# Where the low parts of one weight chunk wait, and split products for six down chunks of the last token block

## The chip, the core and the metric

The kernel runs on one core of a Trainium2 chip. The metric is the device time of one execution in microseconds (us). A core has five engines that run their own instruction queues in order and meet at semaphores: PE (TensorE, the matrix unit), DVE (VectorE), ACT (ScalarE), POOL (GpSimd) and SP (SyncE, which issues DMAs here). PEld is the row of the profile for PE's weight loads.

## The reference

Two stages, one after the other:

```python
def phi(x):                                   # x: (4, 4, 1088, 32), S1, S2: (8, 32)
    a = einsum('rd,bhsd->bhsr', S1, x); b = einsum('rd,bhsd->bhsr', S2, x)
    return einsum('bhsi,bhsj->bhsij', a, b)   # 64 features
q_p, k_p = phi(q), phi(k)
num = q_p @ (k_p^T v);  den = q_p @ sum(k_p) + 1e-6
x = (num / den), heads side by side           # (4352 tokens, 128)
g = x @ w_gate;  val = x @ w_val              # 128 -> 1536
out = (g * sigmoid(g) * val) @ w_out          # 1536 -> 128
```

The feed-forward part is what this text is about: for every block of tokens, 1536 hidden columns in 12 chunks of 128, each made by a gate and a value product, and then a down product of each chunk with `w_out`, summed over the 12 chunks.

## The kernel before, in words

Tokens are cut into blocks: three of batch 0 (numbers 0, 1, 2, of 384, 320 and 384 tokens), then `line`, six blocks of 480 and a last one, `LAST`, of 384. A unit (i, j) is chunk j of block i: gate and value product, silu on ACT, and on DVE the product of both into a slot of `hbuf` (or `late`). A down (i, j) multiplies that slot by chunk j of `w_out` into a PSUM bank that gathers the block's 12 chunks. `todo` holds the units whose down is still to come.

Blocks 0 and 1 use plain float32 products (line 1016). From block 2 on the gate and value products are split: an operand is cut into parts that fit float32r, one matmul instruction each, and a product is the sum of three. The weights' parts are made by `cut_weights` (line 839), a generator that does one step each time it is advanced: `w1` on ACT (line 843); the low part `low = w - w1` into room lent to it, on POOL or DVE (line 846); `wb`, the scaled low part, on ACT (line 848); `wd`, their difference, on POOL or DVE (lines 851, 855). Four chunks of three (0 to 3) of `wg` and `wv` are cut, under the names g0 to g3 and v0 to v3; g0 and v0 use POOL. `steps_at` tables (lines 1307, 1328, 1343, 1355) say by hand after which unit or down each step is issued. A unit of a split block is `start_unit` (line 974: two matmuls with `wd`, then ACT rescales both banks in place, line 983) and `finish_unit` (line 985: four matmuls, lines 992 and 993, silu at line 995, DVE's product at line 1000). Three PSUM pairs serve these units; `let_go` frees one after line 1000.

Around the first edit: in lines 1333 to 1340 thirteen downs are issued (`ND`), with cuts between them; lines 1347 to 1353 run units (2, 6) to (2, 11), one unit ahead on PE, with one down after each and one step of batch 1's attention (`parts_of`, lines 377, 741 to 758). That attention ends in `phT`, which PE needs at line 776 before the next blocks' tokens exist. v0's low part goes to `room[:, 6]` and g0's to `room[:, 8]`, which are free long before; ACT instructions and POOL instructions are queued in the order in which the program issues them.

Around the second edit: `DOWN` (lines 888, 889) lists the downs that are split as well: six of `line[2]` and eight each of `line[3:6]`. For such a unit `cut_hidden` (line 942) makes three parts of the hidden chunk: h1 one step later (ACT, line 959, or DVE, line 957), h0 two steps later on POOL (line 960), hd three steps later on DVE (line 963). `before` and `behind` are lists by step y that `finish_unit` runs at its begin and at its end. `down` (line 1045) then issues three float32r matmuls (lines 1060, 1062, 1063) in place of one plain float32 product, which is two instructions (line 1068). The sum of the `wd` products and the plain chunks lies in one bank; the other two parts lie in a second bank `p`, which ACT copies to SBUF (`copy_out`, line 1081) and DVE joins with the first (`put_together`, line 1088, line 1092). In a block with split downs the plain chunks use `scaled`, a copy of `-w_out` (line 930) that holds the seven chunks in `PLAIN`. `LAST` has none of this: its downs cover 256 tokens (`SPLIT`), all plain, and are stored by a DVE transpose (line 1113) and four DMAs on two queues; the other 128 tokens are done by `straight` (line 1097), the operands exchanged, at the very end, and leave through `o_last`.

The loop over `line` (lines 1381 to 1399) issues at step y the start of unit y+1, the finish of unit y and up to two downs:

```python
        for _ in range(2):
            if len(todo) > min(5 + (todo[0] == (line[1], 0)), END - y + 1):
                down(y)
```

Of the kernel before, what the change touches and what calls it, by code (L numbers as in the profile page):

```python
# [12 lines left out]
AF = mybir.ActivationFunctionType  # L13
# [6 lines left out]
def kernel(  # L20
# [818 lines left out]
    def cut_weights(w, c, low, engine):  # L839

        w1, wb, wd = w_parts[id(w), c] = home(w, c)
        src = w[:, 3 * c : 3 * c + 3, :]
        nc.scalar.activation(out=w1, in_=src, func=AF.Copy, scale=CUT)
        yield
        low = low[0]
        engine.tensor_tensor(out=low, in0=src, in1=whole(w1), op=ALU.subtract)
        yield
        nc.scalar.activation(out=wb, in_=low, func=AF.Copy, scale=BETA)
        yield
        if engine is nc.vector:  # L850
            nc.vector.scalar_tensor_tensor(
                out=wd, in0=low, scalar=-BETA, in1=whole(w1), op0=ALU.mult, op1=ALU.add
            )
        else:
            engine.tensor_tensor(out=wd, in0=whole(w1), in1=whole(wb), op=ALU.subtract)

    def cut_tokens(i, engine=nc.gpsimd, soon=False):

        t0, n = blocks[i]
        x = xT[:, t0 : t0 + n]  # L860
        x1, x0, xd = x_parts[i] = [
            apool.tile([P, WB], F32R, tag=tag, name=name, bufs=2)
            for tag, name in (("qb", "x1"), ("dT", "x0"), ("rd", "xd"))
        ]
        nc.scalar.activation(x1[:, 0:n], x, AF.Copy, scale=CUT)  # L865

        def low():
            engine.tensor_tensor(  # L868
                out=x0[:, 0:n], in0=x, in1=whole(x1[:, 0:n]), op=ALU.subtract
            )  # L870

        def difference():
            nc.vector.scalar_tensor_tensor(
                out=xd[:, 0:n], in0=whole(x1[:, 0:n]), scalar=WHOLE, in1=x,
                op0=ALU.mult, op1=ALU.subtract,
            )


        first, second = (difference, low) if soon else (low, difference)
        first()  # L880
        yield
        second()
# [1 line left out]


    line = list(range(HEAD, len(blocks)))
    FINE, PLAIN = range(1, NCH - 1), (0, 1, 3, 5, 7, 6, NCH - 1)
    DOWN = [(line[2], j) for j in (2, 4, 6, 8, 9, 10)]
    DOWN += [(i, j) for i in line[3:6] for j in (1, 2, 4, 5, 7, 8, 9, 10)]
    down_parts = {}  # L890
    h_parts = {}
    h_sets = []
# [2 lines left out]
    def add_to(where, y, f):  # L895
        where.setdefault(y, []).append(f)
# [5 lines left out]
    def cut_down():  # L902

        n = len(FINE)
        parts = const.tile([P, 3, n, D], F32R, tag="room", name="dparts", bufs=1)
        w1, wb, wd = (parts[:, k] for k in range(3))
        scaled = apool.tile([P, len(PLAIN), D], FP32, tag="zs", name="scaled")
        low = const.tile([P, n, D], FP32, tag="late", name="dlow", bufs=1)
        down_parts.update(w1=w1, wb=wb, wd=wd, scaled=scaled)
        rest = [(0, slice(0, 1)), (1, slice(1, 8, 2)), (5, slice(6, 7)), (6, slice(NCH - 1, NCH))]  # L910

        def high(c):
            nc.scalar.activation(w1[:, c], wo[:, FINE[0] :][:, c], AF.Copy, scale=CUT)

        def left(c):
            nc.gpsimd.tensor_tensor(
                out=low[:, c], in0=wo[:, FINE[0] :][:, c], in1=whole(w1[:, c]), op=ALU.subtract
            )

        def scale(c):  # L920
            nc.scalar.activation(wb[:, c], low[:, c], AF.Copy, scale=BETA)

        def differ(c):
            nc.gpsimd.tensor_tensor(
                out=wd[:, c], in0=whole(w1[:, c]), in1=whole(wb[:, c]), op=ALU.subtract
            )

        def other(k, c):
            m = len(range(NCH)[c])
            nc.scalar.activation(scaled[:, k : k + m, :], wo[:, c, :], AF.Copy, scale=-1.0)  # L930

        a, b, c = slice(0, 3), slice(3, 6), slice(6, n)
        for step in (
            [(high, a)], [(left, a), (high, b)], [(left, b), (scale, a)], [(differ, a), (high, c)],
            [(left, c), (scale, b)], [(differ, b), (scale, c)], [(differ, c), (other, *rest[0])],
            [(other, *rest[1])], [(other, *rest[2]), (other, *rest[3])],
        ):
            for f, *args in step:
                f(*args)
            yield  # L940

    def cut_hidden(y, i, j):

        if not h_sets:
            x = []
            for tag in ("kld", "qld", "vld", "kT", "qT"):
                t = const.tile([P, 2, WB], F32R, tag=tag, name="h" + tag, bufs=1)
                x += [t[:, k, :] for k in range(2)]
            t = const.tile([P, 8, WB], F32R, tag="late", name="hlate", bufs=1)
            x += [t[:, k, :] for k in range(8)]  # L950
            h_sets.extend(x[k : k + 3] for k in range(0, 18, 3))
        n = blocks[i][1]
        h_sets.append(h_sets.pop(0))
        h1, h0, hd = h_parts[i, j] = [x[:, 0:n] for x in h_sets[-1]]
        h = hidden[i, j][:, 0:n]
        if j in (2, 5, 8, 10) and i != line[2]:
            add_to(before, y + 1, lambda: nc.vector.tensor_scalar(h1, h, CUT, None, op0=ALU.mult))
        else:
            add_to(behind, y + 1, lambda: nc.scalar.activation(h1, h, AF.Copy, scale=CUT))
        add_to(before, y + 2, lambda: nc.gpsimd.tensor_tensor(  # L960
            out=h0, in0=h, in1=whole(h1), op=ALU.subtract
        ))
        add_to(before, y + 3, lambda: nc.vector.scalar_tensor_tensor(
            out=hd, in0=whole(h1), scalar=WHOLE, in1=h, op0=ALU.mult, op1=ALU.subtract
        ))
# [115 lines left out]
    def copy_out(y, i, n):  # L1081

        x = fpool.tile([P, WB], FP32, tag="sg", name="sum2", bufs=5)[:, 0:n]
        p = acc[i, "p"][:, 0:n]
        acc[i, "p"] = x
        add_to(behind, y + 1, lambda: nc.scalar.activation(x, p, AF.Copy, scale=WHOLE))

    def put_together(y, i, n):

        d, x = acc.pop(i)[:, 0:n], acc.pop((i, "p"))  # L1090
        acc[i] = x
        add_to(before, y + 1, lambda: nc.vector.scalar_tensor_tensor(
            out=x, in0=d, scalar=-1.0, in1=x, op0=ALU.mult, op1=ALU.add
        ))
        add_to(before, y + 2, lambda: store(i, n))

    def straight(ps, j):

# [10 lines left out]
    def store(i, n):  # L1109
        t0 = blocks[i][0]  # L1110

        o = fpool.tile([P, WB // 32, 32], FP32, tag="o", name="o", bufs=2)
        nc.vector.transpose(
            out=o[:, 0 : n // 32, :], in_=acc.pop(i)[:, 0:n].rearrange("p (x t) -> p x t", t=32)
        )
        t1 = t0 + n
        while t0 < t1:
            b, x0 = divmod(t0 // 32, NX)
            m = min(t1 - t0, S * (b + 1) - t0) // 32
            k = (t0 - blocks[i][0]) // 32  # L1120
            for a in range(4):
                queue = nc.scalar if i == LAST and a % 2 else nc.sync
                queue.dma_start(
                    out=rows[b, a, :, x0 : x0 + m, :],
                    in_=o[32 * a : 32 * a + 32, k : k + m, :],
                )
            t0 += 32 * m
# [106 lines left out]
    def parts_of(n):  # L1234

        for _ in range(n):
            if ahead[0] not in ("pe", "end"):
                ahead[0] = next(att, "end")
# [37 lines left out]
    def free(c):  # L1276
        return [room[:, c, :].rearrange("p (c f) -> p c f", f=P)]
# [11 lines left out]

    cuts = {"x": cut_tokens(2, nc.vector, soon=True)}
    for c in (2, 3, 0, 1):
        cuts["g%d" % c] = cut_weights(wg, c, free(8 + c % 2), nc.vector if c else nc.gpsimd)
        cuts["v%d" % c] = cut_weights(wv, c, free(6 + c % 2), nc.vector if c == 1 else nc.gpsimd)

    def at(*names):
        for name in names:
# [9 lines left out]
    for z, (i, j) in enumerate(seq):  # L1308
# [18 lines left out]

    steps_at = {
        0: ("g2", "v2", "v3"), 1: ("g2",), 2: ("g2", "g3"), 3: ("g3", "v2"), 4: ("g3", "v3"), 5: ("g2",),
        7: ("x",), 8: ("x", "g3", "v0"), 9: ("g0",), 10: ("v0",), 11: ("g0",),  # L1330
    }
    ND = 13
    for n in range(ND):
# [7 lines left out]


    steps_at = {
        9: ("v0",), 10: ("g0", "v0"), 11: ("g0", "v1", "g1", "v1", "g1"),
    }
    todo.sort(key=lambda x: (order + [x]).index(x))
    for j in range(6, NCH):
        if j + 1 < NCH:
            start_unit(2, j + 1)
        finish_unit(2, j)  # L1350
        next_down()
        parts_of(1)
        at(*steps_at.get(j, ()))
    x_steps = iter(())
    steps_at = {9: ("v1", "g1"), 8: ("v1", "g1")}
# [87 lines left out]
```

## Time and profile before

| | us |
|---|---|
| median of 3 runs (277.64 to 278.03) | 277.65 |
| the profiled execution's own time | 278.16 |
| its span, first to last instruction | 276.5 |
| PE busy in the span | 269.2 |
| DVE busy | 208.4 |
| ACT busy | 189.9 |
| POOL busy | 97.1 |

All is one execution's profile. The span lies inside the measured time: 278.16 - 276.5 = 1.66 us lie around it. A line of the timeline gives start, duration, engine, source line and operation, output and inputs with shape, and in brackets how long the engine stood idle before it and which instruction ended that. A line of the chain gives start, length and what the chain passed through, followed back from the last instruction. Two numbered records make one plain float32 matmul; in a timeline, a matmul's record begins when PE takes it, so that neighbours overlap, and the chain shows the steps without overlap.

### The profile page before, as it was taken

What the parts mean: (1) busy time and instruction counts of PE and PEld (TensorE: products, weight loads), DVE (VectorE), ACT (ScalarE), POOL (GpSimd) and SP (SyncE); (2) the same over time, 40 slices, a digit from 0 to 9 for tenths busy, and PEclk for the clock granted to TensorE, in tenths of its full rate; (3) what the DMA queues carried; (4) which work ended last, traced back from release to release, by engine and by line L of the source; (5) the groups of instructions that cost most, each with busy time, mean ns of one, the idle gap of its engine ahead of it and who ended that gap; (6) DMA issues with size and microseconds to landing.
All of it is one profiled execution on the core that took longest, in us unless ns stands there. A gap on an engine that the chain in (4) does not pass through costs nothing.

```text
span 276.5 us, 5719 instructions
## 1 busy us (share of the span) xinstructions
PE 269.2 (97%) x2181; PEld 199.9 (72%) x2181; DVE 208.4 (75%) x360; ACT 189.9 (69%) x337; POOL 97.1 (35%) x107
## 2 busy tenths in 40 slices
PE   6989999999999999999999999999999999999995
PEld 6645566667785786777577777867887888788994
DVE  2997988989998773887545666967978995987431
ACT  2468666462685686677479898768879878886860
POOL 3323422149611540260043353435425553542000
PEclk9999999999999999999999999999999999999999
DMA  6573196222231043000200020000100200010011
GB/s 190 171 206 93 53 271 195 63 100 63 58 92 20 4 115 94 2 0 0 38 13 4 1 38 0 0 2 13 24 2 0 36 1 0 17 21 0 11 29 29
DMA packets 26139, 14.30 MB, mean 52 GB/s; under 512 B 19840, under 2 KB 24192, under 8 KB 26112
## 3 DMA queue, kind: packets, MB, share of 16 engines
q1 hardware_dynamic: 25456, 13.84, 19.7%
q8 instruction: 17, 0.28, 0.4%
q10 hardware_dynamic: 656, 0.10, 0.2%
q14 instruction: 10, 0.08, 0.1%
HBM read 11.41 MB, written 2.23 MB: 49 GB/s over the span
## 4 chain that ended last, share of the span: by engine, by line
PE 91%; DVE 4%; DMA 2%; issue 1%; ACT 1%; SPq 0%
PE PS L1068 21%; PE PS L980 14%; PE PS L992 14%; PE PS L993 13%; PE PS L1016 12%; PE PS L1063 2%; PE PS L1060 2%; PE PS L1062 2%; PE PS L354 2%; PE PS L776 2%; PE PS L342 2%; DMA kld<-in_k_dram 2%; PE PS L388 2%; PE PS L1099 1%; PE PS L497 1%
## 5 line engine op out<-in xcount | busy, mean ns | idle before, releaser
L983 ACT ACTIVATE PS<-PS 128x960 f32<-128x960 f32 (+1 forms) x90 | 83.3, 925 | 33.7 <-PE PS L980 32.8
L1000 DVE SCALAR_TENSOR_TENSOR hbuf<-PS,sg 128x480 f32<-128x480 f32 (+1 forms) x87 | 55.3, 635 | 43.9 <-ACT sg L995 41.1
L995 ACT ACTIVATE sg<-PS 128x480 f32<-128x480 f32 (+1 forms) x90 | 49.6, 551 | 2.1 <-PE PS L993 1.2
L1068 PE MATMUL PS<-hbuf,wo 128*128 128x480 f32 (+3 forms) x118 | 45.8, 488 | 0.0
L980 PE MATMUL PS<-xd,graw 128*128 128x480 f32 (+1 forms) x69 | 38.2, 554 | 0.0
L993 PE MATMUL PS<-x,wb 128*128 128x480 f32 (+1 forms) x90 | 33.5, 372 | 0.0
L980 PE MATMUL PS<-xd,wd 128*128 128x480 f32 (+1 forms) x90 | 33.5, 372 | 0.0
L992 PE MATMUL PS<-x,w 128*128 128x480 f32 (+1 forms) x90 | 33.4, 371 | 0.0
L1068 PEld LDWEIGHTS PS<-hbuf,wo 128*128 128x128 f32 x118 | 22.0, 189 | 5.6 <-issue 0.4
L993 PE MATMUL PS<-x,graw 128*128 128x480 f32 (+1 forms) x69 | 25.5, 370 | 0.0
L980 PEld LDWEIGHTS PS<-xd,wd 128*128 128x128 f32 x90 | 17.0, 189 | 10.5 <-issue 6.0
L1016 PE MATMUL PS<-xT,wg 128*128 128x384 f32 (+1 forms) x60 | 23.5, 473 | 0.1
L1016 PE MATMUL PS<-xT,wv 128*128 128x384 f32 (+1 forms) x60 | 23.2, 468 | 0.3 <-DVE wv L286 0.3
L868 POOL TENSOR_TENSOR x<-xT,x 128x480 fp32r<-128x480 f32 (+1 forms) x6 | 7.2, 1193 | 38.1 <-ACT x L865 38.1
L1020 ACT ACTIVATE sg<-PS 128x384 f32<-128x384 f32 (+1 forms) x24 | 11.2, 468 | 13.2 <-PE PS L1016 12.4
L980 PEld LDWEIGHTS PS<-xd,graw 128*128 128x128 f32 x69 | 13.0, 188 | 7.7 <-ACT PS L983 4.1
L992 PEld LDWEIGHTS PS<-x,w 128*128 128x128 f32 x90 | 16.9, 187 | 2.2
L993 PEld LDWEIGHTS PS<-x,wb 128*128 128x128 f32 x90 | 16.9, 188 | 2.1
L992 PE MATMUL PS<-x,graw 128*128 128x480 f32 (+1 forms) x48 | 18.4, 384 | 0.0
L1068 PE MATMUL PS<-hbuf,scaled 128*128 128x480 f32 x36 | 17.4, 564 | 0.0
L1016 PEld LDWEIGHTS PS<-xT,wv 128*128 128x128 f32 x60 | 11.2, 190 | 7.3 <-DVE hbuf L1031 0.8
L1016 PEld LDWEIGHTS PS<-xT,wg 128*128 128x128 f32 x60 | 10.9, 190 | 7.7 <-issue 1.1
(200 smaller groups left out, 539.2 us busy)
## 6 DMA issues: line engine op xcount, KB each, us to landing
kld<-in_k_dram SPq DMA_DIRECT2D x4, 544.0 KB, 4.7
vld<-in_v_dram SPq DMA_DIRECT2D x12, 144.0 KB, 4.3
qld<-in_q_dram SPq DMA_DIRECT2D x3, 544.0 KB, 3.6
raw<-in_moe_w_out_dram SPq DMA_DIRECT2D x4, 384.0 KB, 3.9
raw<-in_moe_w_gate_dram SPq DMA_DIRECT2D x3, 384.0 KB, 3.7
raw<-in_moe_w_val_dram SPq DMA_DIRECT2D x3, 384.0 KB, 3.5
out_dram<-o SPq DMA_DIRECT2D x16, 60.0 KB, 1.9
vld<-in_v_dram SPq DMA_DIRECT2D x4, 112.0 KB, 4.0
```

The costliest lines, as they stand in the source:

```text
L342: nc.tensor.matmul(ps[32 * a : 32 * a + 32, 96 * (c - c0) : 96 * (c - c0) + 96], qT[:, 4 * c + a, :], s123[:, a : a + H, :, :].rearrange(" ...
L354: nc.tensor.matmul(ps[32 * a : 32 * a + 64, 64 * (c - c0) : 64 * (c - c0) + 64], kT[:, c, a : a + 2, :].rearrange("p a t -> p (a t)"), s12 ...
L868: engine.tensor_tensor(out=x0[:, 0:n], in0=x, in1=whole(x1[:, 0:n]), op=ALU.subtract)
L980: nc.tensor.matmul(ps[:, k], w_parts[id(w), j // 3][2][:, j % 3, :], xd, start=True, stop=True)
L983: nc.scalar.activation(ps, ps, AF.Copy, scale=-1.0 / WHOLE)
L992: nc.tensor.matmul(ps[:, k], w1, x1, start=False, stop=False, skip_group_check=True)
L993: nc.tensor.matmul(ps[:, k], wb, x0, start=False, stop=True, skip_group_check=True)
L995: nc.scalar.activation(sg, ps[:, 0], AF.Silu, scale=WHOLE)
L1000: nc.vector.scalar_tensor_tensor(out=hj[:, 0:n], in0=ps[:, 1], scalar=WHOLE, in1=sg, op0=ALU.mult, op1=ALU.mult)
L1016: nc.tensor.matmul(o[:, 0:n], w[:, j, :], xT[:, t0 : t0 + n], start=True, stop=True)
L1020: nc.scalar.activation(sg[:, 0:n], g[:, 0:n], AF.Silu)
L1068: nc.tensor.matmul(acc[i][:, 0:n], w, hidden[i, j][:, 0:n], **sides)
```

## The change

Chunk 0 of the weights: v0's low part is no longer put into `room[:, 6]`, but into the slot of `hbuf` that the down of step j = 7 has just freed. Both lows of chunk 0, which were issued at downs 10 and 11 of the thirteen, are issued at that step; both `wb` at step 9 (g0's was at 10), both `wd` at step 10 (g0's was at 11). On POOL the order of the instructions is the same as before; v0's low part now has a wait on PE. On ACT `wb` of g0 stands one unit earlier, ahead of a rescale (line 983) and a silu (line 995).

Last block: the downs of `LAST` for chunks 1, 2, 4, 5, 6 and 7 become split ones, with h parts of 256 tokens; its plain chunks (0, 3, 8, 9, 10, 11) use `scaled`, for which chunks 8, 9 and 10 take the places of 1, 5 and 7 at step 68, by three ACT instructions. The copy of `p`, the join and the store of `LAST` are issued at once rather than one or two steps later.

```diff
-    FINE, PLAIN = range(1, NCH - 1), (0, 1, 3, 5, 7, 6, NCH - 1)
+    FINE, PLAIN = range(1, NCH - 1), [0, 1, 3, 5, 7, 6, NCH - 1]
...
+    DOWN += [(LAST, j) for j in (1, 2, 4, 5, 6, 7)]
...
+        def exchange():
+            for k, c in zip((1, 3, 4), (8, 9, 10)):
+                PLAIN[k] = c
+                nc.scalar.activation(scaled[:, k, :], wo[:, c, :], AF.Copy, scale=-1.0)
+
+        add_to(behind, NCH * 5 + 8, exchange)
...
-        n = blocks[i][1]
+        n = SPLIT if i == LAST else blocks[i][1]
         h_sets.append(h_sets.pop(0))
...
-        add_to(behind, y + 1, lambda: nc.scalar.activation(x, p, AF.Copy, scale=WHOLE))
+        copy = lambda: nc.scalar.activation(x, p, AF.Copy, scale=WHOLE)
+        if i == LAST:
+            copy()
+        else:
+            add_to(behind, y + 1, copy)
...
-        add_to(before, y + 1, lambda: nc.vector.scalar_tensor_tensor(
+        join = lambda: nc.vector.scalar_tensor_tensor(
             out=x, in0=d, scalar=-1.0, in1=x, op0=ALU.mult, op1=ALU.add
-        ))
-        add_to(before, y + 2, lambda: store(i, n))
+        )
+        if i == LAST:
+            join()
+            store(i, n)
+        else:
+            add_to(before, y + 1, join)
+            add_to(before, y + 2, lambda: store(i, n))
...
+    lows = {}
...
-        cuts["v%d" % c] = cut_weights(wv, c, free(6 + c % 2), nc.vector if c == 1 else nc.gpsimd)
+        lows["v%d" % c] = free(6 + c % 2)
+        cuts["v%d" % c] = cut_weights(wv, c, lows["v%d" % c], nc.vector if c == 1 else nc.gpsimd)
...
-        7: ("x",), 8: ("x", "g3", "v0"), 9: ("g0",), 10: ("v0",), 11: ("g0",),
+        7: ("x",), 8: ("x", "g3", "v0"), 9: ("g0",),
...
-        9: ("v0",), 10: ("g0", "v0"), 11: ("g0", "v1", "g1", "v1", "g1"),
+        7: ("v0", "g0"), 9: ("v0", "g0"), 10: ("v0", "g0"), 11: ("v1", "g1", "v1", "g1"),
...
+        if j == 7:
+            lows["v0"][:] = [slots.pop().rearrange("p (c f) -> p c f", f=P)]
         at(*steps_at.get(j, ()))
```

## The prediction

> **What bounds the kernel now.** I read the page first: PE is busy 97% of the span and the chain of work that ended last lies 91% on PE.
>
> ```profile
> PE 269.2 (97%) x2181; PEld 199.9 (72%) x2181; DVE 208.4 (75%) x360; ACT 189.9 (69%) x337; POOL 97.1 (35%) x107
> ...
> PE 91%; DVE 4%; DMA 2%; issue 1%; ACT 1%; SPq 0%
> ```
>
> So an edit pays only where it shortens PE's own work or closes a hole in it. Then I read the chain in the two stretches that the edits touch. First, units (2, 6) to (2, 11), 72 to 98 us:
>
> ```profile
> 80.32 0.55 PE PS L1068 x2
> 80.87 0.01 issue
> 80.88 0.56 DVE late L1000
> ...
> 83.16 0.14 DVE phq L377
> 83.30 1.35 issue
> 84.66 0.54 DVE late L1000
> 85.20 0.90 DVE phT L758
> 86.10 0.04 issue
> 86.14 1.55 PE PS L776 x38
> ```
>
> Up to 80.87 the chain is PE's, 1.58 a unit; from there to 86.14 it is DVE's, through the attention features (line 377) and their transpose (line 758), and PE's line 776 waits for that. PE's timeline tells what the hole costs: its last four downs end at 83.08 + 2.74 = 85.82, line 776 starts at 86.14, idle 0.32. That is the most the first edit can give. Why DVE is late is in its timeline and POOL's:
>
> ```profile
> 72.80 1.29 DVE L1040 TENSOR_TENSOR hbuf<-hbuf,room 128x320 f32<-128x320 f32 x1
> ...
> 79.78 0.95 DVE L377 TENSOR_TENSOR phq<-qab 128x768 f32<-128x768 f32 x1
> ...
> 83.09 1.65 DVE L377 TENSOR_TENSOR phq<-qab 128x768 f32<-128x768 f32 x1
> ```
>
> ```profile
> 71.14 1.32 POOL L846 TENSOR_TENSOR room<-wv,w 128x384 f32<-128x384 f32 x1
> 72.43 1.31 POOL L846 TENSOR_TENSOR room<-wg,gphq 128x384 f32<-128x384 f32 x1
> 81.34 1.01 POOL L855 TENSOR_TENSOR wd<-w,wb 128x384 fp32r<-128x384 f32 x1 [7.59 <-ACT wb L848]
> 82.92 1.00 POOL L855 TENSOR_TENSOR gphq<-gphq 128x384 fp32r<-128x384 f32 x1 [0.57 <-ACT gphq L848]
> ```
>
> The same instruction of line 377 takes 0.95 alone and 1.65 beside g0's `wd` (82.92 to 83.92). It ends at 84.74 and all behind it is 0.70 late. Second, the last block, in the chain from 254 us on:
>
> ```profile
> 255.86 0.22 PE PS L1060
> 256.08 0.22 PE PS L1062
> 256.30 0.22 PE PS L1063
> ...
> 259.41 0.43 PE PS L1068 x2
> ```
>
> The chain stays on PE from 184 us to the end but for the last copy: a down of 480 tokens in three parts takes 0.66, and a plain one of 256 tokens 0.43.
>
> **What the Trainium skill says.** "SBUF — State Buffer", section "Who interferes with whom": a DVE instruction with two SBUF inputs and a GpSimd instruction that reads SBUF exclude each other, and whichever comes second waits for the first to end; with one SBUF input DVE doesn't contend. The trace agrees: 1.65 against 0.95 above, while the transpose at 81.78, one input, takes 0.94 beside POOL's 81.34 to 82.35. "TensorE: Matmul & The Clock Gate", section "LDWEIGHTS (loading the stationary operand)": a load takes its columns divided by 1.2, an estimate of 107 ns for 128 columns. This is a floor for a short matmul if loads run one behind another; the last 16 records (line 1099) take 1.80/16 = 0.113 each, so the trace doesn't contradict it. "FP8 and Floating Point Precision", section "TensorE Precision Notes", says that true float32 takes four passes through the array: the plain down of 256 is 0.43, or 0.107 a pass, and that of 480 0.805, or 0.201, which is 0.42 ns a column in both. No page that I found prices a float32r matmul.
>
> **Part 1, chunk 0's lows.** They leave 71.14 to 73.74 and wait for the down of step 7, which the chain has from 77.16 to 77.70. Removed is a contention that cost nothing: DVE's xd, x and line 1040 took 1.19, 1.36 and 1.29 there, but what follows them waits for the silu of unit 6 (76.1) anyway. Placed anew: alone, POOL takes about 1.0 for 128x384 (both L855), so 77.75 to 78.75 and to 79.75. DVE does line 1000, a transpose and line 1000 there, none with two SBUF inputs, and line 377 starts at 79.78: cost 0, at most 0.1. ACT needs v0's low at 80.73 and g0's at about 81.15, so there is a second of cover and more.
>
> On ACT, g0's `wb` (0.53, about 0.42 from start to start) now stands ahead of the rescale of unit 11 and the silu of unit 10. Rescale: 81.24 becomes 81.6, its end 82.04 becomes 82.4; PE takes unit 11's four matmuls when its down of 384 tokens is through, 81.90 + 0.65 = 82.55. Cost 0, with 0.15 to spare. Silu: its end 82.42 becomes 82.8, and DVE's line 1000 starts at 82.82, not 82.64 (0.18 lost). In return g0's `wd` follows v0's at once on POOL, 82.36 to 83.36, not 82.92 to 83.92. Line 377, at 83.27, is held to 83.36 and ends at 84.31, not 84.74; line 1000 to 84.8, transpose to 85.66. PE is free at 85.82 and finds `phT` ready. The hole of 0.32 is gone; next late is PE itself. What follows (copies of xT, cut of the tokens, first unit of `line`) hangs on line 776 and moves with it. DMAs: the moved steps issue none, and SP's order is unchanged. Value -0.32; bounds -0.32 and 0.
>
> **Part 2, six split downs.** Before: 6 x 0.43 = 2.58. After: 18 float32r matmuls of 256 columns, which the trace doesn't show. Its rows: a unit of six 384-column ones and a plain down of 256 lasts (264.28 - 258.37)/4 = 1.478, less 0.43 is 1.048, or 0.175 each; 480 columns take 0.217 (units of nine, 1.953). The line through both gives 0.119 at 256. From below, a quarter of the plain down, 0.107 (one such pass; also the skill's price of the load); from above, 0.123 if the excess of 384 over four-pass speed (0.175 - 0.161 = 0.014) is a fixed cost, with a little more. I take 0.12: 18 x 0.12 = 2.16, saved 0.42; ends 0.65 and 0.35. All of it is on PE's path.
>
> What the split adds elsewhere, per chunk: a cut (line 959 or 957), a POOL subtraction (line 960) and a DVE difference (line 963). Estimates for 256 columns from 480 and 384: ACT 0.42, DVE 0.3 and 0.4, POOL 0.7. ACT: the rescale of unit y+1 ends about 0.48 before PE wants it (263.98 against 264.46), and had idled 0.28 before; h1 adds some 0.35, so it starts 0.05 to 0.15 late: hidden. If that cover were gone, each of four cuts would cost PE up to 0.35. DVE: line 1000 frees the pair that the start three units later needs (260.59 against 261.34, 0.75 of cover), and DVE is idle 0.8 to 1.3 before most of them; hd may wait 0.7 for POOL and still fit. The tightest is h7's: silu 80 to 264.37, h1 to 264.7, h0 to 265.5, hd after line 1000 of step 81 to 266.9; PE wants it at about 267.3. Cover 0.4. Hidden.
>
> The exchange: three ACT instructions of 128x128, 0.31 each (line 930), at 243.4. They push h1 of line[5]'s chunk 7 and the next rescale by 0.8 to 0.9, from 244.18 to about 245.0; it ends at 245.8 and PE takes it at 245.94. Hidden, by 0.1 to 0.3; with no cover it would cost up to 0.5. POOL's h0 moves behind it and off DVE's cut at 244.29, which took 1.26 for 0.40.
>
> The tail: after the down of chunk 11 (271.39) DVE does a join (about 0.4) and then the transpose; two DMA issues on each queue (0.88) then end 0.4 later, at 273.2, and `o_last` is issued at 273.53. Cost 0, 0.1 if packets queue. The copy of `p` on ACT (0.42) fits between two silus that stand 0.76 idle apart.
>
> **Sum.** 278.16 - 0.32 - 0.42 = 277.42 for the profiled execution, span 275.76 and 1.66 around it. The median of the runs shown is 0.51 below that execution; the same step from 277.65 gives 276.91.
>
> **Rivals.** (a) Only the last block pays: the silu that is pushed back, or POOL's start, leaves `phT` as late as before. For it speaks that my `phT` is only 0.16 before PE is free. 277.65 - 0.42 = 277.23, and 277.5 if the parts price high. (b) Only chunk 0 pays: ACT or DVE in steps 77 to 82 takes back the matmuls' gain, for instance by 0.1 per split chunk over four; 277.65 - 0.32 = 277.33. Against it: idle shares above. (c) Slower: ACT in step 9 waits for POOL. The lows are held by PE, two `wb` stand in ACT's queue ahead of unit 11's rescale, and PE waits for that rescale. It decides from the end of g0's low: at 79.75 there is nothing, past about 81.3 each us is a us of PE. If POOL loses the shared port to DVE more than I think and both lows take 2.3, they end at 82.4: PE stands 1.1, and since the `wd` are then late as well, `phT` loses its gain too; 277.65 + 1.1 - 0.42 = 278.33. For it: these very instructions took 1.3 beside DVE. Against it: they were alone with three two-input DVE instructions then, and now with one. The change does what it says: the matmuls' order names the parts for these six chunks, and a slot is free at that step.
>
> **How the numbers follow.** Both parts 0.56 (276.7 to 277.15), (a) 0.22, (b) 0.10, (c) 0.12. About 0.2%, 0.55 us, is what a measurement of this kernel can tell from no change. Both parts give 0.67 to 0.97, all past it; (a) and (b) 0.15 to 0.5, within it; so faster 0.57, same 0.31, slower 0.12. The time is that of the likeliest, 276.9. The range goes from the price of 0.107 (277.65 - 0.97, 276.65) to (a) at the high price, 277.55, and leaves out (c) and edges.
>
> **What would show it.** Right: no idle before line 776, with line 377's third piece near 0.95 to 1.05; POOL's lows near 77.75 at 1.0 each; three records of 0.12 in place of 0.43 in the last chain, the chain on PE throughout; `o_last` issued some 0.74 earlier. Wrong: an idle PE at unit 11 with ACT's `wb` waiting for POOL; PE waiting for line 983 or for hd in steps 77 to 82; float32r records of 0.14 or more at 256 columns; a rescale that holds PE at step 70.

## The result and the profile after

The changed kernel takes 277.10 us (median of 21 runs, 276.83 to 278.66), the kernel before 277.79 beside it (21 runs): a ratio of 0.9974 with a 95% interval from 0.9962 to 0.9986. That is 0.69 us less where 0.74 was forecast; the interval stands for 0.4 to 1.1 us less, so the time alone tells the change from nothing, but shows neither its parts nor a miss of 0.1. The profiled execution took 276.96, its span 275.2.

The page of the changed kernel, its engines and the shares of its chain:

```profile
PE 269.1 (98%) x2187; PEld 199.8 (73%) x2187; DVE 209.7 (76%) x369; ACT 191.9 (70%) x345; POOL 101.0 (37%) x113
...
PE 93%; DVE 3%; DMA 2%; ACT 1%; issue 0%; SPq 0%
```

PE's share of the chain rose by two points and DVE's fell by one. From line 959 on the lines named here stand 9 to 24 lower in the new file: 983 is now 992, 1000 is 1009, 1060 to 1068 are 1069 to 1077. Lines up to 868 (377, 776, 846, 848, 855) keep their numbers.

The spans can't be subtracted: the first wd matmul of unit (2, 6) starts at 72.91 before and at 72.35 after, though nothing on the chain ahead of it was changed. The first load of k alone takes 4.17 us on the chain, not 4.71. So I measure stretches of the chain that begin and end on PE. S1 runs from that matmul to the first wd matmul of the 480-token blocks (91.13 before, 90.34 after). S2 runs from the wd matmul that starts unit 77 (256.52, 255.71) to the last copy (273.21, 271.99). Units of `line` are numbered by the step y of its loop in which they are finished, so that 72 to 83 are the last block's chunks 0 to 11; unit 10 and unit 11 are (2, 10) and (2, 11). The ends of S1 on the chain, before and then after:

```profile
72.91 0.55 PE PS L980 x2
...
91.13 0.43 PE PS L980 x2
```

```profile
72.35 0.55 PE PS L989 x2
...
90.34 0.44 PE PS L989 x2
```

| kernel | S1 | S2 | median |
|---|---|---|---|
| before | 18.22 | 16.69 | 277.79 |
| changed | 17.99 | 16.28 | 277.10 |

The first edit is worth 0.23, the second 0.41. The whole way from 72 us to the last copy is 200.30 before and 199.64 after, 0.66 less: both edits and 0.02.

The chain of the changed kernel between 71 and 98 us never leaves PE:

```profile
81.34 0.64 PE PS L1077 x2
81.99 0.33 PE PS L1001
82.31 0.17 PE PS L1002
...
82.84 2.58 PE PS L1077 x8
85.42 1.48 PE PS L776 x38
```

The hole before line 776 is gone. But the first matmul of unit 11 (81.99) takes 0.33 on the chain, its neighbours 0.17. That wait is new. DVE's third piece of line 377 and POOL's four instructions, from their timelines:

```profile
82.73 0.95 DVE L377 TENSOR_TENSOR phq<-qab 128x768 f32<-128x768 f32 x1
```

```profile
77.29 1.02 POOL L846 TENSOR_TENSOR hbuf<-wv,w 128x384 f32<-128x384 f32 x1 [6.66 <-PE PS L1077]
78.27 1.03 POOL L846 TENSOR_TENSOR room<-wg,gphq 128x384 f32<-128x384 f32 x1
80.78 1.01 POOL L855 TENSOR_TENSOR wd<-w,wb 128x384 fp32r<-128x384 f32 x1 [1.49 <-ACT wb L848]
81.75 1.01 POOL L855 TENSOR_TENSOR gphq<-gphq 128x384 fp32r<-128x384 f32 x1
```

POOL stands idle for 6.66 us until PE lets the lows go, and they then take 1.02 and 1.03. Both wd are over at 82.76, 0.03 after line 377's piece began, and it takes 0.95 where it took 1.65. ACT's timeline has the price, first the rescale of unit 11 before, then the new order:

```profile
81.24 0.80 ACT L983 ACTIVATE PS<-PS 128x768 f32<-128x768 f32 x1
```

```profile
80.18 0.53 ACT L848 ACTIVATE wb<-hbuf 128x384 fp32r<-128x384 f32 x1
80.59 0.53 ACT L848 ACTIVATE gphq<-room 128x384 fp32r<-128x384 f32 x1
81.01 0.81 ACT L992 ACTIVATE PS<-PS 128x768 f32<-128x768 f32 x1
```

Counted from the first wd matmul of S1, the rescale starts 8.66 us in, not 8.33, and ends 0.34 later than before. It ends at 81.82, and PE takes the matmul that waits for it at 81.87:

```profile
81.18 0.81 PE L1077 MATMUL PS<-hbuf,wo 128*128 128x384 f32 x2
81.87 0.44 PE L1001 MATMUL PS<-x,graw 128*128 128x384 f32 x1
```

In the last block, from the chain's second half:

```profile
258.61 0.43 PE PS L1077 x2
...
260.09 0.12 PE PS L1069
260.21 0.12 PE PS L1071
260.33 0.13 PE PS L1072
...
271.99 0.29 DVE o_last L1430
```

Three records of 0.12 stand where one pair took 0.43, and the chain stays on PE from unit 77 up to the copy.

### The profile page after: what moved, and what is told of

The parts are those of the page before. It is cut to its first block, busy times and chain, and to the rows that moved or that the text cites. A ratio compares the mean times of both kernels' runs of the same rounds, so it can differ in the third digit from the quotient of the medians.

```text
span 275.2 us, 5762 instructions
## 1 busy us (share of the span) xinstructions
PE 269.1 (98%) x2187; PEld 199.8 (73%) x2187; DVE 209.7 (76%) x369; ACT 191.9 (70%) x345; POOL 101.0 (37%) x113
## 4 chain that ended last, share of the span: by engine, by line
PE 93%; DVE 3%; DMA 2%; ACT 1%; issue 0%; SPq 0%
PE PS L1077 21%; PE PS L1001 14%; PE PS L989 14%; PE PS L1002 14%; PE PS L1025 12%; PE PS L1072 3%; PE PS L1069 3%; PE PS L1071 3%; PE PS L354 2%; PE PS L776 2%; PE PS L342 2%; PE PS L388 2%; DMA kld<-in_k_dram 2%; PE PS L1117 1%; PE PS L497 1%; PE PS L445 1%
## 5 line engine op out<-in xcount | busy, mean ns | idle before, releaser
L1077 PE MATMUL PS<-hbuf,wo 128*128 128x480 f32 (+2 forms) x94 | 39.4, 516 | 0.0
L1077 PEld LDWEIGHTS PS<-hbuf,wo 128*128 128x128 f32 x94 | 17.6, 189 | 5.4 <-issue 0.4
L1077 PE MATMUL PS<-hbuf,scaled 128*128 128x480 f32 (+1 forms) x48 | 20.6, 518 | 0.0
L969 POOL TENSOR_TENSOR hlate<-hbuf,hlate 128x480 fp32r<-128x480 f32 (+1 forms) x12 | 14.3, 1198 | 11.3 <-ACT hlate L968 9.2
```

The lines of the kernel that those rows point to most:

```text
L969: add_to(before, y + 2, lambda: nc.gpsimd.tensor_tensor(out=h0, in0=h, in1=whole(h1), op=ALU.subtract))
L1077: nc.tensor.matmul(acc[i][:, 0:n], w, hidden[i, j][:, 0:n], **sides)
```

## The experiments

The theory after the result: the two edits add; the first closes a hole of 0.32 because g0's wd runs earlier, and opens a wait of 0.16 because g0's wb stands ahead of a rescale; the hold on the lows does nothing. Rivals: the hold is what helps; the wait at unit 11 has another cause; the edits need each other.

**Each edit alone.** First the chunk-0 part of the diff alone on the kernel before, then the rest of it alone.

> Only the first edit (chunk 0's lows held to step 7, both wb at step 9, both wd at step 10); the last block as before. I measure two stretches of the chain: S1 from the first wd matmul of unit (2, 6) to that of the first unit of the 480-token blocks (before 91.13 - 72.91 = 18.22 us, after 90.34 - 72.35 = 17.99), and S2 from the wd matmul that starts unit 77 (256.52 before, 255.71 after) to the last copy (before 273.21 - 256.52 = 16.69, after 271.99 - 255.71 = 16.28). Theory (the parts add, and the first is worth less than forecast because the rescale of unit 11 now makes PE wait about 0.16): S1 17.99, S2 16.69, time 0.23 below before. Forecast as on record: S1 17.90, 0.32 below. Rival (the first edit does nothing alone): S1 18.2, time as before.

Measured: S1 18.00, S2 16.70; median 277.44 against 277.75, ratio 0.9988 (0.9979 to 0.9996).

> Only the second edit (six split downs of the last block, with the exchange and the direct store); chunk 0 as before. Theory: S1 18.22 as before, S2 16.28, 18 float32r matmuls of 256 columns at 0.12 each, time 0.42 below before. Rival (the parts need each other, or ACT and DVE take part of it back): S2 16.4 or more, time 0.3 below or less.

Measured: S1 18.22, S2 16.28; median 277.34 against 277.75, ratio 0.9984 (0.9972 to 0.9995). Each stretch moves with its own edit alone, and ACT and DVE take nothing back. The two ratios multiply to 0.9972, against 0.9974 for the changed kernel; that agrees with parts that add, but the intervals are too wide to show it. The stretches do.

**Without the hold.**

```diff
-            lows["v0"][:] = [slots.pop().rearrange("p (c f) -> p c f", f=P)]
+            pass
```

> The changed kernel with one line less: v0's low part goes to its old room, so nothing holds the two lows back on POOL; the steps are issued as in the changed kernel. Theory (the hold itself is worth nothing; what counts is that g0's wd runs earlier than the third piece of line 377): POOL's lows start near 71 us again, DVE's xd, x and line 1049 take 1.2 to 1.4 there, the third piece of line 377 stays at 0.95 and S1 at 17.99 within 0.03. Rival (the hold keeps DVE early enough and is what closes the hole): S1 18.1 or more, an idle before line 776.

Measured: S1 18.00, S2 16.28, median 277.15, ratio 0.9974 (0.9964 to 0.9984). POOL's timeline of this kernel:

```profile
70.85 1.32 POOL L846 TENSOR_TENSOR room<-wv,w 128x384 f32<-128x384 f32 x1
72.14 1.32 POOL L846 TENSOR_TENSOR room<-wg,gphq 128x384 f32<-128x384 f32 x1
```

The lows are back beside DVE's x (1.36) and line 1049 (1.29), and nothing is lost: the third piece of line 377 takes 0.95 all the same. The hold, from which the change has the first half of its name, is worth nothing in this stretch.

**g0's wb and wd late again, the hold kept.**

```diff
-        7: ("v0", "g0"), 9: ("v0", "g0"), 10: ("v0", "g0"), 11: ("v1", "g1", "v1", "g1"),
+        7: ("v0", "g0"), 9: ("v0",), 10: ("v0", "g0"), 11: ("g0", "v1", "g1", "v1", "g1"),
```

> The changed kernel with g0's wb and wd one step later, at 10 and 11 as before the change; the lows stay held to step 7. Theory (g0's wb ahead of the rescale costs 0.16 and buys the gap on POOL): the first matmul of unit 11 waits no more, but g0's wd meets the third piece of line 377 again, which takes 1.4 to 1.7, and the hole before line 776 is back: S1 18.2. Rival (the hold alone closes the hole): S1 17.85 to 18.0.

Measured: S1 18.23, from one execution (277.50). POOL's, DVE's and PE's timelines of this kernel:

```profile
82.68 1.00 POOL L855 TENSOR_TENSOR gphq<-gphq 128x384 fp32r<-128x384 f32 x1 [0.58 <-ACT gphq L848]
```

```profile
82.85 1.65 DVE L377 TENSOR_TENSOR phq<-qab 128x768 f32<-128x768 f32 x1
```

```profile
85.91 1.49 PE L776 MATMUL PS<-phT,spread 32*32 32x288 f32 x58 [0.32 <-DVE phT L758]
```

The 1.65 is back, and 0.32 of idle before line 776 with it, as PE's timeline, the last of the three, has it; unit 11's matmul waits no more. So the place of g0's wb and wd, one unit earlier or later, is the whole effect of the first edit, its gain and its price.

**One wb a step.**

```diff
-        7: ("v0", "g0"), 9: ("v0", "g0"), 10: ("v0", "g0"), 11: ("v1", "g1", "v1", "g1"),
+        7: ("v0", "g0"), 8: ("v0",), 9: ("g0", "v0"), 10: ("g0",), 11: ("v1", "g1", "v1", "g1"),
```

> The changed kernel with one wb a step: v0's wb at step 8, g0's at step 9, v0's wd at 9, g0's at 10. Theory (two wb ahead of unit 11's rescale make PE wait 0.16): with one there is no wait, the silu of unit 10 is not pushed back, no wd meets line 377's third piece: S1 17.83, 0.16 below the changed kernel. v0's wd may be held for line 377's second piece, which costs nothing. Rival (PE's 0.16 at unit 11 has another cause): S1 17.99. Rival (ACT waits for v0's low at step 8 and pushes the rescale of unit 10): S1 18.1 or more.

> The spread kernel again, beside the changed kernel on one chip: S1 17.84 and S2 16.28 as in its first run. Theory (0.15 us less on PE's chain is a gain that the median can only just show): median 0.1 to 0.2 below the changed kernel's. Rival (the start of the program, up to the first wd matmul, varies more than that): medians within 0.1 of each other or in reverse, with S1 and S2 unchanged.

> The changed kernel again, on the chip of the two runs beside it, as their measure: S1 17.99, S2 16.28, 0.65 to 0.75 us below before.

> The changed kernel beside the spread one: S1 17.99, S2 16.28.

Measured: S1 17.84 in both runs of this kernel (called the spread kernel from here on) and 17.99 in both of the changed kernel; S2 16.28 in all four. The wait at unit 11 is gone and the hole stays closed, as the chain of the second run shows:

```profile
82.20 0.17 PE PS L1001
...
85.48 1.48 PE PS L776 x38
```

v0's wd is held for line 377's second piece and takes 1.79 on POOL; nobody waits for that. Medians: 277.29 beside 277.13 in the first pair (22 and 5 runs), 276.96 beside 277.07 in the second (11 and 20). The gain of 0.15 is shown on the chain, and the medians, which point one way in the first pair and the other in the second, do not settle it: the first profile of the spread kernel came to its first wd matmul at 73.81, the second at 72.57, so the start alone varies by more. Against the kernel before, S1 is 0.38 shorter.

**g0's wb done twice.** One ACT copy repeated (lines shift by one).

> The changed kernel with g0's wb done twice, so that ACT has 0.42 more ahead of unit 11's rescale. Theory (the cover is used up, each 0.1 on ACT is 0.1 on PE): the first matmul of unit 11 is held 0.42 longer, 0.58 in all, S1 18.41, no idle before line 776. As the record had it (0.15 to spare with one wb): 0.27 in all, S1 18.2. Rival (the wait at unit 11 isn't the rescale): S1 17.99 to 18.05.

The second copy into the same place took more than the first; the rescale now starts 0.56 later than in the changed kernel, counted from the first wd matmul, not 0.42. PE's timeline of this kernel:

```profile
82.55 0.44 PE L1002 MATMUL PS<-x,graw 128*128 128x384 f32 x1 [0.44 <-ACT PS L993]
```

S1 is 18.54, from one execution (277.63), 0.55 more than in the changed kernel. (This kernel's chain does not pass through the start of S1, so the start is PE's timeline plus 0.07, the difference that the changed kernel has there.) The wait is for the rescale, and with g0's wb ahead of it the cover is used up: 0.56 more on ACT was 0.55 more on PE.

**The exchange done twice.** The three `scaled` copies at step 68 repeated, ahead of unit 70's rescale.

> The changed kernel with the exchange's three ACT copies done twice: about 0.60 more ahead of unit 70's rescale, which then ends at about 245.23 on the clock of the changed kernel's profile, while PE's slot for unit 70's first matmul is at 245.29. I measure S3, from the wd matmul that starts unit 69 (240.78) to that of unit 76 (253.99): 13.21 in both kernels so far. Theory (PE wants the rescale about 0.32 before the slot, the 0.05 of the semaphore and 0.27 of a matmul that can't be filled behind its forerunner): 0.26 lost, S3 about 13.47. Rival (the cover ends at the slot itself, as the prediction counted): S3 13.21 to 13.25.

One execution (277.81). Here too repeated copies took longer (six in 1.74, three in 0.71), so the rescale ends 1.03 later, not 0.60. S3 is 254.87 - 240.98 = 13.89, 0.68 lost. In the changed kernel the rescale had ended 0.66 ahead of its matmul's slot, the place that the matmul has on the chain when it waits for nothing (244.63 against 245.29). Of that only 1.03 - 0.68 = 0.35 was cover: PE wants the rescale 0.31 ahead of the slot. The rival, with the copies as slow as they were, would have lost 0.37. PE's timeline of this kernel shows a matmul for which PE stood idle, 0.48 from begin to end, where 0.22 is its step on the chain:

```profile
245.92 0.48 PE L1002 MATMUL PS<-x,graw 128*128 128x480 f32 x1 [0.42 <-ACT PS L993]
```

**Seven split downs.** The spread kernel with chunk 3 of the last block in `DOWN` too.

> The spread kernel with chunk 3 of the last block split too (seven split downs). Theory: S1 17.83, and S2 16.28 - (0.43 - 0.36) = 16.21; time about 0.23 below the changed kernel. Rival (ACT is full: the h part of chunk 3 stands beside the copy of the block before, and pushes a rescale): S2 16.28 or more.

Measured: S1 17.84, S2 16.30; median 277.22 beside 277.29 of the spread kernel and 277.13 of the changed one. No gain. The chain of this kernel has the start of unit 81:

```profile
261.88 0.43 PE PS L989 x2
```

It takes 0.43 here, and 0.34 to 0.36 for the units around it. It needs a bank pair that DVE must have left, and DVE's timeline has line 1009 late:

```profile
261.27 0.54 DVE L1009 SCALAR_TENSOR_TENSOR hbuf<-PS,sg 128x384 f32<-128x384 f32 x1
```

In the changed kernel the one that frees this pair, unit 78's, begins 1.21 ahead of the start (260.65 against 261.86); here it is 0.61 ahead (261.27 against 261.88) and ends at 261.81, behind an hd that POOL held to 0.89, a transpose and a cut. So the place where it broke is DVE, not ACT as my rival had it. That the 0.08 is this wait is read from the trace; no run takes it away.

## Why the prediction was right

**Which work pays** held: both gains lie where the chain said, and between 91 us and unit 77 nothing moved beyond 0.02. The time came out nearer to the forecast than the working was: the stretches give 0.64, not 0.74, and nearly all that is missing is missing in Part 1.

**Part 1** was right in its mechanism and too large by 0.09: 0.23, not 0.32. Held: the lows cost nothing where they now lie (1.02 each, line 377's second piece at 0.95), the contention at 71 us was free (the run without the hold), the wd of g0 was what made `phT` late, and nothing late follows. (The 1.19 of DVE's xd, which I counted to that contention, stands in the changed kernel too, beside an earlier wd on POOL; only x and line 1040 got faster, to 0.55 and 0.48.)

The term that failed is "Cost 0, with 0.15 to spare", for g0's wb ahead of unit 11's rescale. I had counted the cover up to the matmul's slot, 82.55. It ends about 0.3 sooner: from the rescale's end to PE's taking of the matmul it is 0.05 (81.82 to 81.87), and a matmul for which PE had to wait lasts 0.44 to its end at 384 columns, 0.27 more than its step of 0.17. So of the 0.51 of cover (82.04 to 82.55) about 0.2 was real, and moving the rescale by 0.34 cost 0.16. Line 776 gave 0.07 back, since it now follows the downs without a break and takes 1.48 on the chain, not 1.55; 0.32 - 0.16 + 0.07 is the 0.23. I had called 0.32 the most that the first edit can give; with that 0.07 it is more, and the spread kernel has 0.38. `phT` was to be 0.16 ahead of PE and is 0.38 ahead (85.04 against 85.42), in part because PE itself is 0.16 late.

**Part 2** held to the hundredth: 0.12 for a float32r matmul of 256 columns, which no row had shown, from the line through 384 and 480; 0.41 saved of 0.42. The 0.113 of line 1099 could not test the estimate for a weight load that stood at the lower end of that price: such a record is half a plain float32 product, two passes of 128 columns, and 0.107 by the 0.42 ns a column that the prediction works out. The profile's own records of such loads last 0.19 each and start 0.12 apart in the split downs, so they overlap, and the 107 ns are neither shown nor refuted here. The cuts hid as forecast: ACT's h1 took 0.42, POOL's h0 0.74, and DVE's hd 0.41 alone and 0.89 where POOL was first.

The exchange was hidden (S3 is 13.21 in both kernels), but with some luck. I took its three copies at 0.31 each, a push of 0.8 to 0.9 on the rescale of unit 70, and the cover as ending at 245.94, when PE takes the matmul. The copies start 0.20 apart (three in 0.71) and pushed the rescale by 0.29, counted from the start of S3 (2.88 against 2.59); 0.35 of cover was left. With the push that I forecast the rescale would have ended at 245.8, and the cover ended at 246.10 - 0.31 = 245.79: nothing to spare. Two terms were off, and the one made up for the other.

The tail was free: the join took 0.42, and `o_last` was issued 0.32 after its copy began, as before. Counted from the first wd matmul of S1 that is 0.66 earlier, where 0.74 was forecast.

One sum was off and moved nothing: 277.65 - 0.97 is 276.68, not 276.65.

**The rivals.** (a) and (b) failed with the two single edits, which both pay. (c) needed lows that end past 81.3 on the clock of before; they ended at 79.30, which is 79.86 on that clock, and ACT never waited for them. That ACT would hold PE at unit 11 was (c)'s place, but the cause was ACT's own queue, not POOL.

## What to carry to other kernels

Count cover up to the moment when PE must take an instruction, not up to the slot that it has on the chain when nothing holds it: here 0.3 us less. An instruction in the profile that takes nearly twice its usual time beside another engine can be worth more than its share of busy time says, if a wait hangs on it; ask which of the two could run a unit earlier, and what then stands ahead of what in the third engine's queue. When a change has several parts under one name, undo them one at a time: the part that named this one did nothing.

## What the runs showed of the hardware

A float32r matmul of 256 columns steps at 0.12, of 384 at 0.175, of 480 at 0.217; that is 0.013 to 0.016 above a quarter of a plain float32 product of the same size (0.107, 0.161 and 0.201). A PE matmul for which PE stood idle lasts 0.44 from begin to end at 384 columns, where its step is 0.17, and 0.48 at 480, where it is 0.22: 0.26 to 0.27 more. The profile models the ends of matmuls, so these two alone would be weak; the losses in S1 and S3 carry it.

Not expected: an ACT copy repeated right behind itself took longer. Two wb into two places hold ACT for 0.83 up to the next rescale (80.18 to 81.01), two into one place for 0.98 (80.72 to 81.70); three `scaled` copies hold it for 0.60, six for 1.64, not 1.20. Both are about 0.15 for each repetition, a little more than the 0.11 to 0.12 by which such copies overlap in the profile when each has its own place (0.53 long and 0.41 apart, 0.31 and 0.20). The repeated copy writes the place that its forerunner wrote and also reads the place that it read; which of the two makes it slow, and whether by a wait, no run asks.

Between DVE and POOL either may lose: line 377 went from 0.95 to 1.65 behind a wd, and a wd from 1.01 to 1.79 behind line 377, as the Trainium skill has it in "SBUF — State Buffer", section "Who interferes with whom": whichever comes second waits.
